# A full-width stationary for the d = 0 column, a planner without a chain of loads and with new lengths, and the third batch's folds five units later

## The chip, the cores and the metric

The kernel runs on one core of a Trainium2 chip. The metric is the device time of one execution in microseconds (us), the median of several runs. TensorE is called PE, VectorE DVE, ScalarE ACT, GpSimd POOL and SyncE SP, as in the profile.

## The reference, cut to what matters

```python
def attn(x):                       # x: (8, 3008, 256) float32
    X = np.fft.fft(x, axis=1)
    X = np.fft.fft(X, axis=2)
    return X.real                  # 24064 rows of 256

def moe(x, w_gate, w_val, w_out):  # 256 -> 1536 -> 256
    g = x @ w_gate
    silu = g * (1.0 / (1.0 + np.exp(-g)))
    val = x @ w_val
    return silu * val @ w_out
```

The output is `moe(attn(x))` in float32. Nothing but the real part of the two-dimensional transform is needed, so the kernel works with cosine and sine tables as matrix products.

## The kernel before, in words

**Folding.** The sequence transform has symmetries in both axes. POOL adds and subtracts rows of `x` (function `fold_steps`, lines 150 to 176) so that a batch is left as small coefficient tiles: `CEa` and `BBa` for the first 128 rows of a quarter (kind "A", written to one of two buffers called `cp`), and `Fc` for the remaining 60 (kind "C", for two batches at a time), which SP's DMAs spread into the stacked tile `St`. One set of folds of a kind has 12 steps, six for each `q`. Kind A reads the tile `XA`, kind C the tile `XC`; both are loaded from HBM by SP, `XA` by 20 DMAs per batch (lines 131 and 133), `XC` by 20 per batch (lines 140, 142 and 144).

**Transform.** For each of eight batches `b`, `transform_op` (line 1296) multiplies the coefficients with the tables `Tab` on PE. Part 0 has 377 output columns and part 1 has 376; each part is done for `eo` = 0 and 1, each with a product for `q` = 0 into an `o` tile in PSUM and one for `q` = 1 into a `g` tile. ACT copies the first (`od`), DVE adds and subtracts (`put`) and so writes columns of `Pt` and `Qt`, 512 columns in a tile, 24 tiles.

The column d = 0 has one coefficient more than fits in 128, so in part 0 with `eo` = 1 the function `row0` (line 586) adds three further matmuls to output row 0 alone, for each `q`: their stationary operand is 128 rows by 1 column, and they write `ps[0:1, ...]`.

**The feed-forward part.** Work goes in units `(t, f)`: tile `t` of 24, and block `f` of 12 of the 1536 hidden features, 288 units in all. In a unit PE multiplies `Pt` and `Qt` with the transformed weights `Wp`, `Wq` and `Wm` (`mm`, line 937) into the PSUM tiles `g` (gate) and `v` (value), three buffers each. Each tile also serves the mirrored rows. In the first tiles most units are "whole": DVE takes the two products with ACT's SiLU. Elsewhere they are "split": `es` (even part of the value; DVE line 1060, or ACT line 1058) and `sg` (of the gate, DVE line 1039), then `sv` (DVE line 1121 and ACT line 1107), `hp` on DVE (line 1131) and, for two units together, `hm` on POOL (`product_m`, line 1128). `es` and `sg` on DVE need a row of `Qt` spread over all partitions: for each tile, SP's DMA writes it to `br` (line 1448) and a second one to `bc` (line 1456). `OWork` multiplies `hp` and `hm` of the tile before with `Wo` (line 1177), ACT evicts (lines 1183 and 1186) and SP stores (line 1189).

**The order.** After a prologue of some 22 us, nothing is issued directly. `S.add` (line 776) records each operation with its engine, a length `dur`, the keys that it reads and writes, and a place `at`, which is the sum of PE's lengths so far plus a `shift`. A write depends on the last write of the same key and on all reads since then, and then forgets those reads. `S.run` (line 802) plays the operations in time: on each engine it takes, among those within a window of the earliest one left (2 us of `at` for PE and ACT, 3 for DVE and SP, 6 for POOL), the one that can start first. What comes out is only an order of instructions for each engine; on the chip the engines wait on semaphores. Lengths are formulas: `pe_us`, `act_us`, `dve_us` and constants.

Each of the 20 loads of `XA` for batch 1 was given, besides its own key, a write of a common one:

```python
w=[((what[0],), k)] + ([(("A",), "pre" if k > 15 else "preW")] if what == ("A", 1) else []), lat=LOAD_LAT)
```

Those two keys stand for the data that lie in the same memory before: `preW` for the raw weights, read by `weight_op`, and `pre` for angles, read by `angle_op` and `sine_op`. A load is given 10 us of latency (`LOAD_LAT`).

`spread` (line 1219) lays the 12 steps of a fold over a stretch of units. Batch 1 has its C folds in units 6 to 14 and its A folds in 15 to 24; for batch 2 the C folds went to units 25 to 44 and the A folds to 45 to 63. Transforms have a unit of their own: 33 for (batch 1, part 0), 64 for (2, 0), 88 for (3, 0), and `eo` = 1 comes one unit later.

Of the kernel before, what the change touches and what calls it, by code (L numbers as in the profile page):

```python
# [14 lines left out]
BF16 = mybir.dt.bfloat16  # L15
# [16 lines left out]
def kernel(  # L32
# [8 lines left out]
    nc = tc.nc  # L41
    B, M, D = x.shape
    Dff = moe_w_gate.shape[1]
    P = 128
    H = M // 2
    G = M // 8
# [15 lines left out]
    NCE = 2 * GH + 1  # L62
# [33 lines left out]
    SDt = const.tile([P, 2, P], BF16, name="SDt")  # L96
    m2 = const.tile([P, 1], F32, name="m2")
    mM = const.tile([P, 4], F32, name="mM")
    wC = const.tile([P, 1], F32, name="wC")
    sgn = const.tile([P, 1], F32, name="sgn")  # L100
    XA = const.tile([P, 8, 2, D], F32, name="XA")
# [85 lines left out]
    def coef_a(b):  # L187
        if b not in coefA:
            coefA[b] = (cp.tile([P, 2, 2, 2, P + 1], BF16, name="CEa"),
                        cp.tile([P, 2, 2, 2, P], BF16, name="BBa"))  # L190
        return coefA[b]
# [43 lines left out]
    q = nc.sync  # L235
# [349 lines left out]

    def row0(b, q, ps):
        CE = coef_a(b)[0]
        todo = [(CE[:, q, 0, k, P:P + 1], Tab[:, 0, q, 0, e], e) for k, e in ((0, E0), (1, E1))]
        if b:
            todo.append((stack_of(b, 0)[:, q, 0, P:P + 1], Tab[:, 1, q, 0, 0:NCE], slice(0, NCE)))  # L590
        else:
            todo += [(CEc[:, q, 0, k, 0:1], Tab[:, 1, q, 0, e], e) for k, e in ((0, E0), (1, E1))]
        for l, r_, cols in todo:
            nc.tensor.matmul(ps[0:1, cols], l, r_, start=False, stop=True, skip_group_check=True)

# [134 lines left out]
    LOAD_LAT = 10.0  # L730
# [34 lines left out]
    class Sched:  # L765
# [7 lines left out]
        def hold(self, *owner):  # L773
            self.live[owner[0]].append(owner)

        def add(self, eng, dur, fn, r=(), w=(), new=(), lat=None, shift=0.0):
            o = Op()
            o.eng, o.dur, o.fn, o.n = eng, dur, fn, len(self.ops)
            o.lat = LAG[eng] if lat is None else lat
            o.at = self.clock + shift  # L780
            if eng == "PE":
                self.clock += dur
            o.new, o.deps, o.owners = list(new), set(), set()
            for k in r:
                o.owners.add(k[0])
                if k in self.wr:
                    o.deps.add(self.wr[k])
                same = self.rd.setdefault(k, [])
                if k[0][0] in PSUM:
                    o.deps.update(x for x in same if self.ops[x].eng != eng)  # L790
                same.append(o.n)
            for k in w:
                o.owners.add(k[0])
                if k in self.wr:
                    o.deps.add(self.wr[k])
                o.deps.update(self.rd.pop(k, ()))
                self.wr[k] = o.n
            o.deps.discard(o.n)
            o.owners.update(o.new)
            self.ops.append(o)  # L800
# [96 lines left out]
        return n / 1200 + 0.055  # L897

    def dve_us(n):
        return n / 960 + 0.072  # L900

    def pool_us(n):
        return 0.16 + 1.76e-3 * n
# [109 lines left out]
    def part_a(u):  # L1013
        if whole(u):
            return whole_a(u)
        t, f = u
        w = width(t) + (B if t == nT - 1 else 0)
        kg, kv, kP, kQ = unit_keys(u)
        ksp, kes, keg = (("sp", u), 0), (("es", u), 0), (("sg", ("eg", u)), 0)
        kb = (("bc", t), 0)  # L1020

        def h():
            if t not in hts:
                hts[t] = (hp.tile([P, nF, T + B], BF16, name="hp"), hp.tile([P, nF, T], BF16, name="hm"))

        def g1():
            T_[kg] = psG.tile([P, T], F32, name="g")
            mm(T_[kg], Wp, 0, u, pq_tiles(t)[0], w, True, False)

        def g2():  # L1030
            mm(T_[kg], Wq, 0, u, pq_tiles(t)[1], w, False, True)

        def silu():
            T_[ksp] = spp.tile([P, T], F32, name="sp")
            nc.scalar.activation(T_[ksp][:, :w], T_[kg][:, :w], AF.Silu)  # L1035

        def even_gate():
            T_[keg] = sgp.tile([P, T], F32, name="sg")
            nc.vector.scalar_tensor_tensor(T_[keg][:, :w], bc[t][:, :w], w0[:, 0, f:f + 1], T_[kg][:, :w],  # L1039
                                           op0=Alu.mult, op1=Alu.add)  # L1040

        S.add("PE", pe_us(w), g1, r=[kP], w=[kg], new=[("g", u)])
        if gate_split(u):
            S.add("DVE", dve_us(w) + 0.075, even_gate, r=[kb, kg, (("w0",), 0)], w=[keg], new=[keg[0]], shift=SH_EG)
        else:
            S.add("PE", pe_us(w), g2, r=[kQ], w=[kg])
            S.add("ACT", act_us(w), silu, r=[kg], w=[ksp], new=[ksp[0]], shift=SH_SP)
        ahead = seeded(u)

        def v1():  # L1050
            if not ahead:
                T_[kv] = psV.tile([P, T], F32, name="v")
            mm(T_[kv], Wp, 1, u, pq_tiles(t)[0], w, not ahead, False)

        def even_value():
            T_[kes] = esp.tile([P, T], F32, name="es")
            if ahead:
                nc.scalar.copy(T_[kes][:, :w], T_[kv][:, :w])  # L1058
            else:
                nc.vector.scalar_tensor_tensor(T_[kes][:, :w], bc[t][:, :w], w0[:, 1, f:f + 1], T_[kv][:, :w],  # L1060
                                               op0=Alu.mult, op1=Alu.add)

        S.add("PE", pe_us(w), v1, r=[kP], w=[kv], new=[("v", u)])
        if ahead:
            S.add("ACT", act_us(w) - 0.015, even_value, r=[kv], w=[kes], new=[kes[0]], shift=SH_ES)
        else:
            S.add("DVE", dve_us(w) + 0.075, even_value, r=[kv, kb, (("w0",), 0)], w=[kes], new=[kes[0]], shift=SH_ES)

    def part_b(u):
        if whole(u):  # L1070
# [150 lines left out]

    spread(("C", 1), 12, 6, 14)
    spread(("A", 1), 12, 15, 24)
    lo = 25
    for b in range(2, B, 2):
        u = slot[(b, 0)] - 1
        spread(("C", b), 12, lo, (lo + u) // 2)
# [10 lines left out]
    def run_loads(n):  # L1238
        for what, k, fn in loads[:n]:
            S.add("SP", (0.33 if k < 16 else 0.62) if what[0] == "A" else (0.33 if k % 20 < 15 else 0.9), fn,  # L1240
                  w=[((what[0],), k)] + ([(("A",), "pre" if k > 15 else "preW")] if what == ("A", 1) else []), lat=LOAD_LAT)
        del loads[:n]

    FOLD = (("X", "F"), ("F", "E"), ("F", "O"), ("EO", "A"), ("A", "CE"), ("EO", "BB"))
# [2 lines left out]
    def fold_step(what, i, unit):  # L1247
        kind, b = what
        q, j = divmod(i, 6)
        if i == 0:  # L1250
            run_loads(max((k + 1 for k, (w_, _, _) in enumerate(loads) if w_ == what), default=0))

        def fn():
            if j == 0:
                if kind == "A":
                    queue[what] = fold_steps(nc.gpsimd, XA, *coef_a(b), q, slice(0, P))
                else:
                    if q == 0:
                        foldC[b] = fcp.tile([P, 2, 4 * ND], BF16, name="Fc")
                    F5 = foldC[b].rearrange("p k (q e n) -> p q e k n", q=2, e=2)  # L1260
                    queue[what] = fold_steps(nc.gpsimd, XC, F5[..., 0:NE], F5[..., NE:ND], q,
                                             slice(64 if b == 1 else 0, P))
            queue[what].pop(0)()

        dst = ("cp", b) if kind == "A" else ("fc", b)
        tmp = ("fold",)
        r = {0: [((kind,), k) for k in range(40)], 1: [(tmp, "F")], 2: [(tmp, "F")], 3: [(tmp, "E"), (tmp, "O")],
             4: [(tmp, "A")], 5: [(tmp, "E"), (tmp, "O")]}[j]
        w = {0: [(tmp, "F"), (tmp, "E")], 1: [(tmp, "E")], 2: [(tmp, "O")], 3: [(tmp, "A")],
             4: [(dst, (q, 0))], 5: [(dst, (q, 1))]}[j]  # L1270
        S.add("POOL", FOLD_US[j], fn, r=r, w=w, new=[dst], shift=SH_FOLD)
        if q == 1 and j == 0:
            act_at.setdefault(max(unit + LOAD_AT, 15), []).append(what)
        if kind == "C" and q == 1 and j == 5:
            spread_at[unit + 2] = b

    def load_next(what):
        kind, b = what
# [17 lines left out]
    def transform_op(b, part, eo):  # L1296
# [3 lines left out]
        kd = (("od", (b, part, eo)), 0)  # L1300
        coef = [(("cp", b), (q, part)) for q in range(2)] + [(("st", b), k) for k in range(2)]
        coef += [(("Tab",), k) for k in ((("o", 0), ("o", 1)) if not b else ("k", "z"))]
        us = 0.5 if part == 0 else 0.42
        extra = 0.2 if part == 0 and eo else 0.0
        S.add("PE", us + extra, todo["q0"], r=coef, w=[ko], new=[ko[0]])
        S.add("ACT", act_us(n), todo["od"], r=[ko], w=[kd], new=[kd[0]], shift=SH_OD)
        S.add("PE", us + extra, todo["q1"], r=coef, w=[kg], new=[kg[0]])
# [101 lines left out]
    def rows_op():  # L1409
# [9 lines left out]
        S.add("PE", 0.7, product, r=[(("Wq",), (fc, gv)) for fc in range(1, 3) for gv in range(2)], w=[ko], new=[ko[0]])  # L1419
        S.add("ACT", 0.15, lambda: nc.scalar.copy(w0.rearrange("p g f -> p (g f)"), T_[ko][:, 0:2 * nF]), r=[ko], w=[(("w0",), 0)])  # L1420

    def halve_tables():
        nc.gpsimd.memset(Tab[0:64, 1, :, :, GH + 1:NCE], 0.0)
        nc.gpsimd.memset(Tab[64:P, 1, :, :, 0:GH + 1], 0.0)
# [6 lines left out]
    def odd_op(i):  # L1431
# [3 lines left out]
              4: [lambda: weight_op(2, 0), lambda: angle_op(1)], 5: [lambda: weight_op(2, 1), lambda: cosine_op(1)],  # L1435
              7: [lambda: sine_op(0), rows_op], 8: [lambda: sine_op(1)], 9: [weigh_op],
              13: [lambda: odd_op(0)], 14: [lambda: odd_op(1)], 15: [lambda: odd_op(2)], 16: [lambda: odd_op(3)],
              17: [lambda: S.add("POOL", 0.8, halve_tables, w=[(("Tab",), "z")])]}

    def row_width(t):  # L1440
        return width(t) + (B if t == nT - 1 else 0)
# [115 lines left out]
```

## Time and profile before

| | |
|---|---|
| median of 3 runs | 612.57 us (612.53 to 613.61) |
| span of the profiled execution | 611.4 us, 12521 instructions |
| PE busy | 599.6 us (98%) |
| DVE busy | 581.1 us (95%) |
| ACT busy | 526.4 us (86%) |
| POOL busy | 470.8 us (77%) |
| granted PE clock | 1.000 |

The profile is of one execution, and gives its span from the first to the last instruction; no time of its own stands beside it. The median of the runs is 1.2 us above that span, and what lies around the span is taken to stay the same. Matmuls overlap in the records, so a busy PE need not be one at its peak; the starts of its matmuls tell more.

### The profile page before, as it was taken

The page shows a single profiled execution, that of the slowest core. Times are in us where ns is not written, and L with a number is a line of the kernel's source. Part 1 is how long each engine was busy: PE and PEld are TensorE (multiplying, and loading weights), DVE is VectorE, ACT ScalarE, POOL GpSimd, SP SyncE. Part 2 cuts the span into 40 slices and gives each one's busy share as a digit, 9 for nine tenths or more (in the row PEclk, how much of TensorE's full clock was granted, in tenths as well). Part 3 has the DMA queues.
Part 4 walks back from the last instruction along what each step waited for, and adds up shares of the span by engine and source line. Part 5 has one row for each costly group of instructions (what it writes and reads, how often), then busy time and mean ns, then how long its engine had stood idle before and what let it go on. Part 6 is the DMA issues. An engine that isn't in the chain of part 4 may idle for free. (4 is left out here: it accounts for less than half of the span.)

```text
span 611.4 us, 12521 instructions
## 1 busy us (share of the span) xinstructions
PE 599.6 (98%) x4028; PEld 394.2 (64%) x4088; DVE 581.1 (95%) x1073; ACT 526.4 (86%) x1003; POOL 470.8 (77%) x427
## 2 busy tenths in 40 slices
PE   8999999999999999999999999999999999999997
PEld 6555666666666666666666666666666666666686
DVE  8999899999999999999999999999999999999992
ACT  7686567999989889889999899998898988999994
POOL 8869999999787999977987869867886444446652
PEclk9999999999999999999999999999999999999999
DMA  9957447445425223464152113134211111111212
GB/s 226 144 100 137 126 112 172 116 139 129 133 53 150 70 65 105 136 130 132 45 155 79 54 45 96 53 92 127 62 55 43 49 59 47 51 43 55 59 53 79
DMA packets 50736, 57.71 MB, mean 94 GB/s; under 512 B 7256, under 2 KB 37724, under 8 KB 50670
## 3 DMA queue, kind: packets, MB, share of 16 engines
q1 hardware_dynamic: 47016, 53.78, 33.3%
q0 software_dynamic: 3216, 2.36, 2.9%
q10 hardware_dynamic: 438, 0.77, 0.5%
q8 instruction: 32, 0.52, 0.4%
q14 instruction: 34, 0.28, 0.2%
HBM read 29.43 MB, written 24.65 MB: 88 GB/s over the span
## 5 line engine op out<-in xcount | busy, mean ns | idle before, releaser
L1128 POOL TENSOR_TENSOR hm<-sv 128x1024 bf16<-128x1024 f32 (+2 forms) x135 | 251.0, 1860 | 112.0 <-ACT sv L1107 63.7
L1121 DVE SCALAR_TENSOR_TENSOR sv<-es,v 128x512 f32<-128x512 f32 (+2 forms) x270 | 181.4, 673 | 2.8 <-PE v L937 1.7
L1131 DVE TENSOR_TENSOR hp<-sp,v 128x512 bf16<-128x512 f32 (+2 forms) x264 | 177.7, 673 | 3.9 <-ACT sp L1104 2.1
L1177 PE MATMUL o<-Wo,hm 128*128 128x256 bf16 (+1 forms) x1128 | 167.1, 273 | 0.6
L1177 PE MATMUL o<-Wo,hp 128*128 128x256 bf16 (+1 forms) x1104 | 165.3, 273 | 0.4
L1177 PEld LDWEIGHTS <-hm 128*128 128x128 bf16 (+2 forms) x1140 | 111.9, 98 | 62.0 <-issue 0.2
L1035 ACT ACTIVATE sp<-g 128x512 f32<-128x512 f32 (+2 forms) x205 | 122.6, 598 | 33.0 <-PE g L937 20.7
L1177 PEld LDWEIGHTS <-hp 128*128 128x128 bf16 (+2 forms) x1140 | 112.0, 98 | 58.9 <-issue 1.1
L1107 ACT ACTIVATE sv<-g 128x512 f32<-128x512 f32 (+2 forms) x205 | 133.2, 651 | 8.1 <-PE g L937 3.8
L937 PE MATMUL v<-Pt,Wp 128*128 128x512 bf16 (+2 forms) x283 | 106.2, 375 | 1.3 <-DVE sv L1121 0.4
L1060 DVE SCALAR_TENSOR_TENSOR es<-bc,w,v 128x512 f32<-128x512 bf16 (+2 forms) x144 | 105.5, 734 | 1.2 <-PE v L937 0.8
L937 PE MATMUL g<-Pt,Wp 128*128 128x512 bf16 (+2 forms) x284 | 106.5, 375 | 0.1
L937 PE MATMUL g<-Qt,Wq 128*128 128x512 bf16 (+2 forms) x246 | 92.1, 374 | 0.3
L1009 ACT ACTIVATE v<-bc,w 128x512 f32<-128x512 bf16 (+2 forms) x126 | 86.9, 690 | 0.4
L937 PE MATMUL g<-Qt,Wm 128*128 128x512 bf16 (+2 forms) x215 | 80.6, 375 | 0.4
L1058 ACT COPY es<-v 128x512 f32<-128x512 f32 (+2 forms) x126 | 73.6, 584 | 3.0 <-PE v L937 2.8
L937 PEld LDWEIGHTS <-Wp 128*128 128x128 bf16 x576 | 56.1, 98 | 29.5 <-issue 4.3
L937 PE MATMUL v<-Qt,Wq 128*128 128x512 bf16 (+2 forms) x162 | 60.7, 375 | 2.1 <-DVE es L1060 1.7
L937 PEld LDWEIGHTS <-Wq 128*128 128x128 bf16 x450 | 43.9, 98 | 22.2 <-issue 1.4
L1183 ACT COPY ev<-o 128x512 f32<-128x512 f32 x89 | 53.3, 599 | 4.0 <-PE o L1177 2.7
L937 PE MATMUL v<-Qt,Wm 128*128 128x512 bf16 (+2 forms) x144 | 53.9, 374 | 0.2
L1039 DVE SCALAR_TENSOR_TENSOR sg<-bc,w,g 128x512 f32<-128x512 bf16 (+2 forms) x65 | 47.6, 733 | 1.2 <-ACT sg L972 0.6
(196 smaller groups left out, 682.9 us busy)
## 6 DMA issues: line engine op xcount, KB each, us to landing
out_dram<-ev SPq DMA_DIRECT2D x96, 128.0 KB
XA<-in_x_dram SPq DMA_DIRECT2D x30, 256.0 KB
XA<-in_x_dram SPq DMA_DIRECT2D x112, 64.0 KB
XC<-in_x_dram SPq DMA_DIRECT2D x30, 120.0 KB
XC<-in_x_dram SPq DMA_DIRECT2D x105, 32.0 KB
bc<-br SPq DMA_DIRECT2D x21, 128.0 KB
St<-Fc SPq DMA_DIRECT2D x14, 128.5 KB
out_dram<-ev SPq DMA_DIRECT2D x12, 120.0 KB
```

The source lines that it names most:

```text
L937: nc.tensor.matmul(ps[:, :n], Wt[:, gv, fs], src[:, :n], start=start, stop=stop, skip_group_check=True)
L1009: nc.scalar.activation(T_[kv][:, :w], bc[t][:, :w], AF.Copy, scale=w0[:, 1, f:f + 1])
L1035: nc.scalar.activation(T_[ksp][:, :w], T_[kg][:, :w], AF.Silu)
L1039: nc.vector.scalar_tensor_tensor(T_[keg][:, :w], bc[t][:, :w], w0[:, 0, f:f + 1], T_[kg][:, :w], op0=Alu.mult, op1=Alu.add)
L1058: nc.scalar.copy(T_[kes][:, :w], T_[kv][:, :w])
L1060: nc.vector.scalar_tensor_tensor(T_[kes][:, :w], bc[t][:, :w], w0[:, 1, f:f + 1], T_[kv][:, :w], op0=Alu.mult, op1=Alu.add)
L1107: nc.scalar.activation(sv()[:, f % 2, w - 1::-1, 1], T_[kgm if by_dve else kg][:, :w], AF.Silu)
L1121: nc.vector.scalar_tensor_tensor(sv()[:, f % 2, w - 1::-1, 0], T_[kes][:, :w], 2.0, T_[kv][:, :w], op0=Alu.mult, op1=Alu.subtract)
L1128: nc.gpsimd.tensor_tensor(hts_(t)[1][:, f - 1:f + 1, :w], sv()[:, :, :w, 1], sv()[:, :, :w, 0], op=Alu.mult)
L1131: nc.vector.tensor_tensor(hts_(t)[0][:, f, :wp], T_[ksp][:, :wp], T_[kv][:, :wp], op=Alu.mult)
L1177: nc.tensor.matmul(st["ps"][:n, j, :], hts[t][minus][:, f, c:c + n], Wo[:, f, :], start=(f == 0), stop=(f == nF - 1))
L1183: nc.scalar.copy(ev[:, 0:len(pair), :], st["ps"][:, 0:len(pair), :])
```

## The change

`row0` uses, for every batch but the first, a tile `Z0` of 128 columns per matmul that is zero except for its first column, and writes all 128 rows of the PSUM tile. POOL clears `Z0` once, in unit 6, and copies the coefficients into it after the last A fold of each batch (`d0_op`, two copies per batch). `S.add` gets an argument `after`: it depends on the reads of a key without writing it, and the loads of batch 1 use it in place of the common writes. `dve_us` loses 7 ns and the operations that read `bc` another 15; the lengths of a transform on PE are worked out from its columns. The folds from batch 2 on start at unit 30 where they started at 25, so that the C folds of batch 2 lie in units 30 to 46 and its A folds in 47 to 63.

```diff
+    Z0 = const.tile([P, 2, 3, P], BF16, name="Z0")
...
     def row0(b, q, ps):
         CE = coef_a(b)[0]
+        if b:
+            for k, (c, e) in enumerate(((0, E0), (0, E1), (1, slice(0, NCE)))):
+                nc.tensor.matmul(ps[:, e], Z0[:, q, k, :], Tab[:, c, q, 0, e], start=False, stop=True,
+                                 skip_group_check=True)
+            return
         todo = [(CE[:, q, 0, k, P:P + 1], Tab[:, 0, q, 0, e], e) for k, e in ((0, E0), (1, E1))]
-        if b:
-            todo.append((stack_of(b, 0)[:, q, 0, P:P + 1], Tab[:, 1, q, 0, 0:NCE], slice(0, NCE)))
-        else:
-            todo += [(CEc[:, q, 0, k, 0:1], Tab[:, 1, q, 0, e], e) for k, e in ((0, E0), (1, E1))]
+        todo += [(CEc[:, q, 0, k, 0:1], Tab[:, 1, q, 0, e], e) for k, e in ((0, E0), (1, E1))]
...
-        def add(self, eng, dur, fn, r=(), w=(), new=(), lat=None, shift=0.0):
+        def add(self, eng, dur, fn, r=(), w=(), new=(), after=(), lat=None, shift=0.0):
...
+            for k in after:
+                o.deps.update(self.rd.get(k, ()))
...
     def dve_us(n):
-        return n / 960 + 0.072
+        return n / 960 + 0.065
...
-            S.add("DVE", dve_us(w) + 0.075, even_gate, r=[kb, kg, (("w0",), 0)], w=[keg], new=[keg[0]], shift=SH_EG)
+            S.add("DVE", dve_us(w) + 0.06, even_gate, r=[kb, kg, (("w0",), 0)], w=[keg], new=[keg[0]], shift=SH_EG)
...
-            S.add("DVE", dve_us(w) + 0.075, even_value, r=[kv, kb, (("w0",), 0)], w=[kes], new=[kes[0]], shift=SH_ES)
+            S.add("DVE", dve_us(w) + 0.06, even_value, r=[kv, kb, (("w0",), 0)], w=[kes], new=[kes[0]], shift=SH_ES)
...
-    lo = 25
+    lo = 30
     for b in range(2, B, 2):
...
-                  w=[((what[0],), k)] + ([(("A",), "pre" if k > 15 else "preW")] if what == ("A", 1) else []), lat=LOAD_LAT)
+                  w=[((what[0],), k)], after=[(("A",), "pre" if k > 15 else "preW")] if what == ("A", 1) else [], lat=LOAD_LAT)
...
+        if kind == "A" and q == 1 and j == 5:
+            for part in range(2):
+                d0_op(b, part)
...
-        us = 0.5 if part == 0 else 0.42
-        extra = 0.2 if part == 0 and eo else 0.0
+        us = 3 * 0.0025 + (2 * NCE / 2400 if part == 0 else 3 * G / 2400)
+        extra = us if part == 0 and eo else 0.0
+        if extra:
+            coef += [(("Z0",), k) for k in range(2)]
...
+    def clear_d0():
+        nc.gpsimd.memset(Z0, 0.0)
+
+    def d0_op(b, part):
+        def fn():
+            if part:
+                nc.gpsimd.tensor_copy(Z0[:, :, 2, 0:1], stack_of(b, 0)[:, :, 0, P:P + 1])
+            else:
+                nc.gpsimd.tensor_copy(Z0[:, :, 0:2, 0:1], coef_a(b)[0][:, :, 0, :, P:P + 1])
+
+        r = [(("st", b), k) for k in range(2)] if part else [(("cp", b), (q, 0)) for q in range(2)]
+        S.add("POOL", 0.16, fn, r=r, w=[(("Z0",), part)])
...
+              6: [lambda: S.add("POOL", 0.5, clear_d0, w=[(("Z0",), k) for k in range(2)])]}
```

## The prediction

> **What bounds the kernel now.** I read the page first. PE is the busiest engine:
>
> ```profile
> PE 599.6 (98%) x4028; PEld 394.2 (64%) x4088; DVE 581.1 (95%) x1073; ACT 526.4 (86%) x1003; POOL 470.8 (77%) x427
> ```
>
> Records of matmuls overlap, so I went to the windows to see where PE falls short (columns: window, its length, then busy time of PE, PEld, DVE, ACT and POOL with counts, granted clock, DMA share and GB/s):
>
> ```profile
> 23.00:106.00 83.00, 79.99 (x506) 47.80 (x512) 78.30 (x139) 58.44 (x111) 76.32 (x90) 1.00 0.65 135
> 106.00:579.00 473.00, 470.22 (x3135) 308.67 (x3187) 463.14 (x826) 431.56 (x818) 362.72 (x290) 1.00 0.31 85
> ```
>
> From 106 to 579 us PE lacks 2.8 us of 473, and the list of waits has no row of PE there except its weight loads. I then took starts of matmuls in the timeline. A 512-column matmul is followed by the next start after 216 ns, which is 512 columns at 2.4 per ns plus 2.7 ns; a 256-column one after 109. Wherever the spacing exceeds this by a whole matmul, two weight loads stand in the gap, so a record is missing (60 of 4088 are). What is left in that stretch is one pattern, at the single-column matmuls of line 594:
>
> ```profile
> 424.59 0.32 PE L1320 MATMUL o<-Tab,St 128*128 128x377 bf16 x1
> 424.84 0.33 PE L594 MATMUL o<-Tab,CEa 128*1 128x189 bf16 x2
> 425.01 0.32 PE L594 MATMUL o<-Tab,St 128*1 128x377 bf16 x1
> 425.26 0.39 PE L937 MATMUL v<-Pt,Wp 128*128 128x512 bf16 x1
> ```
>
> A 377-column matmul takes 377/2.4 = 157 ns of array time; from 424.59 to 424.84 is 250 ns, and from 425.01 to 425.26 again. So going into the narrow stationary costs about 95 ns and coming out another 95. Real waits of PE, outside the prologue, are few and early:
>
> ```profile
> PE v L937 <- DVE es L1060: 1.7, 2, 0.9
> PE v L937 <- DVE sv L1121: 0.4, 1, 0.4
> ```
>
> These end at 54.68, 74.02 and 78.68 us. So: PE sets the pace throughout, and only two kinds of time can be won without less work, the switches and the early waits.
>
> **Row 0 with 128 columns.** Seven batches, two `q`: 14 visits. The 14 entries exceed array time by 1.32 us together, the 14 exits by 1.42, of which one (at 93.83) contains 0.08 of another wait. Without a switch each of the 28 steps would still have 3 ns: 0.08. That leaves 1.32 + 1.34 - 0.08 = 2.58 us. What is added: a 128-column weight load in place of a 1-column one (98 against 82 ns in PEld's rows), under short matmuls. The same pair of shapes with 128 columns stands in line 1320: 189 to 188 columns exceeds array time by 3.7 ns, 188 to 377 by 7.2; in line 594 it is 2.3 and 6.1. So 2.5 ns by 14 = 0.04 us. Matmul lengths are equal (243 to 246 ns and 321 in both). Sum **-2.5 us**, all on the path, because no other engine is late in that stretch. Bounds: -2.6 (weight loads quite hidden) and -2.0 (loads exposed by 98 - 79 = 19 ns behind each of the 28 short matmuls, 0.5 us).
>
> The Trainium skill, "TensorE: Matmul & The Clock Gate", section "LDWEIGHTS", speaks against this: a weight load takes the number of columns divided by 1.2, so 107 ns for 128 columns and almost nothing for one. By it a 128-column load under a 78 ns matmul would show 29 ns, an estimate of 0.8 us over 28 short matmuls, and the sum would be -1.7. The trace differs at both ends (82 ns for one column, and 3.7 to 7.2 ns shown at line 1320). For the switch itself, "TensorEngine Tiling (Array Packing)", section "Key Properties", says that changing the tiling mode drains TensorE; the 95 ns agree.
>
> **POOL's copies.** Fourteen small copies; the nearest row is line 557 (`EOA<-SA`, 128x8, 189 ns): 2.6 us of POOL, with 0.5 for clearing `Z0`. The clearing lies in POOL's idle time before 42.27. The copies are in front of PE: row 0 waits for both, and behind them in POOL's queue stand the `hm` products. In the profile of before the last step of batch 2's A folds ends at 148.71 and row 0 starts at 157.16; for batches 3, 4 and 6 the distance is 8 to 9 us too, and larger for 5 and 7. One or two `hm` of 1.85 us each fit between. I take 0; if the copy comes behind two more `hm`, 0 to 2 us at batch 2.
>
> **The planner's loads.** With the common write, each of 16 loads waited in the plan for the load before it, 10.3 us each: some 165 us in a plan where the A folds of batch 1 were meant for units 15 to 24. Loads, folds and all that POOL does behind them were therefore planned far too late, and PE, ACT and DVE were ordered around a stop that the chip never had. On the chip POOL was simply in arrears: it works without a break from 42 to 117 us, and fold steps meant for unit 25 (PE reaches it at 74 us) start at 87.49. Waits of PE between 50 and 106 us, from spacing: 1.00 at 53.46; 0.09 + 1.04 + 0.19 + 0.57 from 72.58 to 78.68; 0.40 in small pieces from 91 to 106. Together 3.3 us, the most that a better order can win. The wait at 53.46 stems from two table copies ahead of `es` on DVE (2.42 us from 51.42, planned at 0.8 each), which the change leaves. The 78.68 one stems from `sv` waiting for POOL's `hm`, whose arrears stay. I take 1.0 of the 1.9 us from 72 to 79: **-1.0**, with 0 to -3.3 as bounds for what is won.
>
> What it costs: SP's order. Before, it was
>
> ```profile
> 35.77 6.96 SPq L131 DMA_DIRECT2D XA<-in_x_dram  x8
> 44.74 0.61 SPq L1448 DMA_DIRECT2D br<-Qt  x1
> 45.40 1.51 SPq L131 DMA_DIRECT2D XA<-in_x_dram  x4
> 47.01 0.61 SPq L133 DMA_DIRECT2D XA<-in_x_dram  x1
> 47.71 0.58 SPq L1456 DMA_DIRECT2D bc<-br  x1
> ```
>
> Free of the chain, all 16 loads of line 131 are due no later than `br` and go first: at 0.87 us each (6.96/8) they end at 49.7, and `bc` moves by up to 5 us, to 52.7. DVE's first `es` started at 53.88; behind `es` on DVE stand `sv` and `hp`, and PE waits for it already. If loads go at the 0.38 us of the second group, nothing is late. I take +0.3, bounds 0 and +2.
>
> **Lengths and unit 30.** The new DVE lengths are 598 ns at 512 columns and 658 with `bc`; starts in the trace are 598 and 658 apart. The plan becomes truer, and nothing changes on the chip except by order. From 106 us there is nothing to win. Moving the folds to unit 30 lets `hm` go first while POOL is in arrears: unit 30 is reached by PE at about 85 us, POOL ends batch 1's folds at 85.69. Four half sets then need about 33 us of folds and 30 of `hm` in 33 units of 2.06 us = 68 us, 93% of POOL; they end near 150, as before. 0 us.
>
> **Sum.** -2.5 - 1.0 + 0.3 = -3.2: a span of 608.2 us where it was 611.4; the median of the runs stands 1.2 above that span, so **609.4 us**.
>
> **Rivals.** (A) *Only the switches go*; the early order merely exchanges one wait for another. For it: the waits stem from POOL's arrears and the table copies, which stay. Time 612.6 - 2.5 = 610.1, up to 611.3 with small new waits. (B) *The row loads come late*: `bc` 5 us later stops DVE's queue at its first `es`, 2 us, and nothing else is won: 612.1; range 611.2 to 613. Against it: those loads were slow only until 43 us. (C) *Slower: DVE loses its margin.* Adding up starts, DVE needs 97 to 98% of each stretch from 98 to 498 us. The old lengths held 27 x 7 + 9 x 22 ns = 0.4 us of reserve per tile (operations of a steady tile); without it the plan lets DVE run later, and if PE waits 0.25 us in each of 21 tiles, that is +5.2: 612.6 - 2.5 + 5.2 = 615.3. It decides from 0.18 us per tile. Against it: PE waits nowhere in 473 us, so order has slack to spare, and the lengths now equal the trace. (D) *The 95 ns do not belong to the column count* but to leaving the product's group or to the small output; then they stay: 612.5. Against: line 1416, also one column, shows 96 and 92 at its ends, while line 1320 to 937 shows 5.
>
> **Chances.** Forecast 0.52, A 0.22, B 0.13, C 0.10, D 0.03. 0.2% is 1.2 us, about what this measurement can tell. Faster: forecast, A and a little of B, 0.76; same: most of B and D, 0.14; slower 0.10. The range starts where all early waits vanish (612.6 - 2.5 - 3.3 = 606.8) and ends at 612.4, within B, leaving out C, D and the end of B.
>
> **What would show it.** Right: line 594 keeps only the prologue's eight narrow matmuls, row 0 follows line 1320 without 95 ns, `PEld L594 <- issue` goes to about 0.5 us; waits of PE from 72 to 79 shrink. Wrong: a PE wait on POOL's `Z0` near a transform, a `bc` landing after 54 us with DVE idle before `es`, or PE waits on `es` and `sv` after 106 us.

## The result and the profile after

The changed kernel is slower, by about as much as the measurement can tell. The median of 20 runs is 615.25 us (613.56 to 618.1), that of the kernel before, timed beside it 20 times, 613.24 us; the ratio is 1.0028, with a 95% interval of 1.0015 to 1.0041. The prediction was 609.4 us with a range of 606.8 to 612.4, so it was wrong in sign, and the time lies above its range. The profiled execution took 616.86 us, 1.76 above its span of 615.1; it is among the longer ones (its granted clock is 0.994, as in 5 others of the 20; 13 have 0.997 and spans of 612.2 to 614.0, one has 0.999).

The head of the page looks harmless (columns as before, and 15 POOL instructions more):

```profile
PE 602.7 (98%) x4088; PEld 397.2 (65%) x4088; DVE 580.3 (94%) x1073; ACT 528.4 (86%) x1003; POOL 473.4 (77%) x442
```

The windows of the changed kernel (length, busy time of PE, PEld, DVE, ACT and POOL with counts, granted clock, DMA share, GB/s) show that the loss lies early. I cut the worst stretch out of the first:

```profile
23.00:106.00 83.00, 76.63 (x477) 45.66 (x476) 73.35 (x130) 55.26 (x104) 70.10 (x85) 0.96 0.60 133
106.00:579.00 473.00, 472.67 (x3194) 311.38 (x3194) 463.42 (x828) 432.41 (x816) 368.29 (x307) 1.00 0.31 85
52.00:57.90 5.90, 0.43 (x3) 0.12 (x2) 0.82 (x2) 1.05 (x3) 5.74 (x7) 0.82 0.31 79
57.90:62.70 4.80, 4.80 (x18) 2.62 (x18) 4.22 (x7) 0.96 (x2) 4.39 (x7) 0.51 0.41 110
```

In the third row PE, DVE and ACT all stand still for more than 4 of 5.9 us; in the fourth PE is fully busy, at half the clock. (The 472.67 of the second row is not better than the 470.22 of before: that trace lacked 60 records of matmuls, this one none.) The list of waits from 23 to 106 us (who waited for whom: us in total, times, the longest) names who was late:

```profile
PE v L942 <- DVE es L1065: 5.5, 1, 5.5
DVE es L1065 <- DMA bc<-br: 5.4, 1, 5.4
```

SP's part of the timeline (start, length, line, transfer, count) shows why `bc` was late. Compare it with the five lines of before in the prediction:

```profile
36.80 10.09 SPq L132 DMA_DIRECT2D XA<-in_x_dram  x16
47.20 2.60 SPq L134 DMA_DIRECT2D XA<-in_x_dram  x4
49.90 0.55 SPq L1472 DMA_DIRECT2D br<-Qt  x1
54.66 0.57 SPq L1480 DMA_DIRECT2D bc<-br  x1
```

All 20 loads now stand ahead of tile 1's row. `br` is issued 5.2 us later (49.90 against 44.74). It also takes longer: `bc`, which waits for its landing, is issued 4.8 us behind it, where it was 3.0 (in e1 and e3 below, 3.5 behind 12 loads and 3.8 behind 20). So `bc` comes 7.0 us later, and DVE's first `es` runs into it, then PE:

```profile
57.08 1.41 DVE L1065 SCALAR_TENSOR_TENSOR es<-bc,w,v 128x512 f32<-128x512 bf16 x2 [5.40 <-DMA bc<-br]
```

```profile
52.03 0.38 PE L942 MATMUL g<-Qt,Wq 128*128 128x512 bf16 x1
57.88 0.58 PE L942 MATMUL v<-Qt,Wq 128*128 128x512 bf16 x1 [5.47 <-DVE es L1065]
58.26 0.63 PE L942 MATMUL v<-Pt,Wp 128*128 128x512 bf16 x1
```

The starts 57.88, 58.26 and 58.69 (the next matmul) are 380 to 430 ns apart, where 512 columns take 216.

What was meant to be won was won. The timeline of PE at a transform after the change has no gap around row 0:

```profile
429.68 0.32 PE L1330 MATMUL g<-Tab,St 128*128 128x377 bf16 x1
429.84 0.49 PE L591 MATMUL g<-Tab,Z 128*128 128x189 bf16 x3
430.17 0.38 PE L942 MATMUL g<-Pt,Wp 128*128 128x512 bf16 x1
```

From 429.68 to 429.84 is 160 ns for 157 of array time, where it was 250.

**Where the time went.** For each kernel in the table I added up what the starts of PE's matmuls exceed their array time (columns / 2.4 per ns, plus 2.6 ns). "Rest" is the span without the prologue, whose length varies by itself between 21.8 and 23.4 us. The other columns are its excess in us: the switches into and out of narrow stationaries, the extra of matmuls at half clock (told by their doubled spacing where the granted clock is down), and waits by stretch of time. `e1` and so on are the experiments below.

```
kernel            span   rest   switches half  <50  50-70 70-106 106-580 >580
before           611.36 588.83   2.69   0     2.02  1.00  2.26   0.08   0.17
after            615.09 593.19   0.09   2.09  2.11  5.82  0.69   1.92   0.02
e1_loads11       610.69 588.68   0.09   0     2.01  0.40  3.84   1.86   0.02
e2_z0            609.49 587.22   0.09   0     2.07  0.56  2.78   1.20   0.08
e3_nochain       616.38 594.59   2.69   1.68  2.54  5.63  1.17   0      0.24
e4_chain         611.41 589.12   0.09   0     2.03  1.46  3.28   1.81   0.02
e5_len           612.06 589.69   2.69   0     2.06  0.49  3.25   0.78   0.02
e6_lo30          611.53 589.24   2.70   0     2.35  1.25  2.08   0.06   0.18
e13_oldlen       608.97 586.16   0.09   0     2.33  1.44  0.82   1.15   0.08
e15_halve6       611.00 588.44   0.09   0     2.04  0.28  3.90   2.10   0.02
e16_z0_halve6    610.68 587.25   0.09   0     2.03  1.49  1.93   1.17   0.08
```

After less before, in the two profiled executions: switches -2.60, waits from 50 to 70 us +4.82, half clock +2.09, 70 to 106 us -1.57, 106 to 580 us +1.84, the end -0.15, prologue -0.63, all else -0.1: +3.7 us. The medians differ by 2.0 only; that most executions have a clock of 0.997 and not 0.994 fits that.

### The profile page after: what moved, and what is told of

Same layout as the page of the kernel before. It is cut to its first block, busy times and chain, and to the rows that moved or that the text cites. A ratio compares the mean times of both kernels' runs of the same rounds, so it can differ in the third digit from the quotient of the medians.

```text
span 615.1 us, 12630 instructions
## 1 busy us (share of the span) xinstructions
PE 602.7 (98%) x4088; PEld 397.2 (65%) x4088; DVE 580.3 (94%) x1073; ACT 528.4 (86%) x1003; POOL 473.4 (77%) x442
## 4 chain that ended last, share of the span: by engine, by line
PE 90%; DMA 3%; ACT 3%; DVE 3%; issue 1%; SPq 0%; POOL 0%; ACTq 0%; DVEq 0%
PE o L1182 37%; PE g L942 26%; PE v L942 19%; PE o L1330 2%; PE g L1330 2%; DMA XC<-in_x_dram 1%; DMA XA<-in_x_dram 1%; DMA br<-Qt 1%; ACT sp L1040 1%; ACT sv L1112 1%; PE v L1182 1%; DVE hp L980 0%; DVE sv L1126 0%; DVE hp L1136 0%; ACT v L1014 0%
## 5 line engine op out<-in xcount | busy, mean ns | idle before, releaser
L1112 ACT ACTIVATE sv<-g 128x512 f32<-128x512 f32 (+2 forms) x205 | 135.5, 662 | 17.0 <-PE g L942 16.8
L1040 ACT ACTIVATE sp<-g 128x512 f32<-128x512 f32 (+2 forms) x205 | 125.0, 610 | 21.8 <-PE g L942 21.2
L942 PE MATMUL v<-Pt,Wp 128*128 128x512 bf16 (+2 forms) x288 | 108.1, 375 | 0.3 <-DVE hm L1000 0.2
L942 PE MATMUL g<-Pt,Wp 128*128 128x512 bf16 (+2 forms) x288 | 108.1, 375 | 0.0
L942 PE MATMUL g<-Qt,Wq 128*128 128x512 bf16 (+2 forms) x288 | 108.0, 375 | 0.0
L942 PE MATMUL g<-Qt,Wm 128*128 128x512 bf16 (+2 forms) x223 | 83.7, 375 | 0.6 <-ACT sp L1040 0.4
L1109 ACT ACTIVATE sp<-g 128x512 f32<-128x512 f32 (+2 forms) x65 | 38.3, 590 | 13.1 <-DVE sg L1104 13.1
```

What stands on the lines that cost most here:

```text
L942: nc.tensor.matmul(ps[:, :n], Wt[:, gv, fs], src[:, :n], start=start, stop=stop, skip_group_check=True)
L1109: nc.scalar.activation(T_[ksp][:, :wp], T_[kg][:, :wp], AF.Silu)
L1112: nc.scalar.activation(sv()[:, f % 2, w - 1::-1, 1], T_[kgm if by_dve else kg][:, :w], AF.Silu)
```

## The experiments

Each was timed in five rounds against the kernel before.

**Put the row's place back: e1.** Theory 1: the order of SP's queue is all that is wrong, and the loss is `bc`. The changed kernel, with eight of batch 1's 20 loads given to the planner later:

```diff
-        if i == 8:
+        if i == 11:
             loads[0:0] = ... load_a(1, ...)
```

> The changed kernel, with the loads of batch 1's XA entering the plan at unit 11 where they enter at 8; in SP's order twelve loads then stand ahead of tile 1's br and bc, and eight behind. Theory 1 (tile 1's row is late because 20 loads stand ahead of it; PE waits 5.6 us and then runs some 5 us at half clock): the wait falls to 1 us or so, the clock stays at 1.000, the span goes from 615.1 to about 608.5, 3 us under the kernel before. Theory 2 (the new order itself is worse, by its lengths and by the folds from unit 30, with some 2.4 us of small waits of PE between 106 and 579 us): the long wait goes too, but the span stays at 611 or above, no better than before.

Median 612.28 against 613.2, ratio 0.999 (0.9966 to 1.0014). SP's timeline in this kernel:

```profile
36.72 8.51 SPq L132 DMA_DIRECT2D XA<-in_x_dram  x12
45.69 0.61 SPq L1472 DMA_DIRECT2D br<-Qt  x1
49.14 0.63 SPq L1480 DMA_DIRECT2D bc<-br  x1
```

The long wait and the half clock are gone: 7.5 us less in the table's two columns. So the cause of the early loss is the queue's order. But only 4.4 us of span came back, less than theory 1 asked for, because a wait of 2.5 us appeared at 75.68 that neither kernel had in that length. In the timeline of e1:

```profile
73.19 2.35 POOL L158 TENSOR_TENSOR SDf<-XA 128x1020 f32<-128x1020 f32 x1
...
75.65 1.89 POOL L1133 TENSOR_TENSOR hm<-sv 128x1024 bf16<-128x1024 f32 x1
...
77.58 1.29 DVE L1126 SCALAR_TENSOR_TENSOR sv<-es,v 128x512 f32<-128x512 f32 x2 [2.33 <-POOL hm L1133]
78.32 0.38 PE L942 MATMUL v<-Pt,Wp 128*128 128x512 bf16 x1 [2.36 <-DVE sv L1126]
```

Read upwards: PE waits for `sv` on DVE, that for a buffer which `hm` on POOL must free, and `hm` stands behind a fold step of batch 1. This is POOL's arrears, which the prediction knew (in the kernel before, the wait at this place was 0.57 us). In the changed kernel it does not show: POOL worked 5.74 of the 5.9 us in which PE stood still. That POOL caught up by this was read from the trace, not tested; e13 below shows that POOL's lateness alone does not make the 2.5 us.

**Each part alone: e3, e2, e5, e6.** The kernel before, with only `after=` in place of the common writes:

```diff
+            for k in after:
+                o.deps.update(self.rd.get(k, ()))
...
-                  w=[((what[0],), k)] + ([(("A",), ...)] if what == ("A", 1) else []), lat=LOAD_LAT)
+                  w=[((what[0],), k)], after=[(("A",), ...)] if what == ("A", 1) else [], lat=LOAD_LAT)
```

> The kernel before with the planner's loads freed of their chain, nothing else. Theory 1: the long wait for tile 1's row is there in full, 5 to 6 us with a clock under 1 behind it, the waits from 72 to 79 us are gone, and the time is 3 to 6 us above the kernel before. Theory 2: without the new lengths and unit 30 there is little harm: within 1.5 us of the kernel before.

Median 617.0 against 613.2, ratio 1.0043 (1.002 to 1.0067): this part alone costs 0.4%, as theory 1 expected (3.8 us). Its `br` and `bc` come later still than in the changed kernel, and PE's clock falls in the same way (SP's timeline, then the window behind the wait):

```profile
48.77 2.61 SPq L133 DMA_DIRECT2D XA<-in_x_dram  x4
51.48 0.54 SPq L1450 DMA_DIRECT2D br<-Qt  x1
55.29 0.57 SPq L1458 DMA_DIRECT2D bc<-br  x1
```

```profile
58.50:63.00 4.50, 4.46 (x17) 2.55 (x17) 4.26 (x7) 1.31 (x3) 4.09 (x5) 0.53 0.40 109
```

Compared with the kernel before, ACT's order of instructions is the same, and PE's differs in 32 places, DVE's in 7, POOL's in 8 and SP's in 11 of its 626 transfers. So the false chain had shaped few places of any order but SP's. One of them counts. In the kernel before, PE lost 1.04 us to `es` at 74.02:

```profile
74.02 0.38 PE L937 MATMUL v<-Qt,Wq 128*128 128x512 bf16 x1 [0.88 <-DVE es L1060]
```

This wait, 1.04 us each time, and one of 0.18 to 0.19 us some 2 us behind it stand in all six kernels that keep the chain and the old `SH_FOLD` (before, e2, e4, e5, e6, e16). In the seven without the chain (the changed kernel, e1, e3, e7, e8, e13, e15) neither is there.

Only row 0 with `Z0` (`row0`, `clear_d0`, `d0_op` and the dependency of the transform on it):

```diff
+        if b:
+            ... nc.tensor.matmul(ps[:, e], Z0[:, q, k, :], ...)
+            return
```

> The kernel before with the 128-column stationary alone (tile Z0, its clearing and its copies on POOL); the planner, its lengths and unit 25 as before. Theory 1 and theory 2: 2.5 us faster than before (28 switches of 95 ns gone), with PE's early waits where they were. If the 95 ns do not belong to the column count: no difference. If POOL's copies stand in front of PE: slower, with a PE wait at a transform.

Median 612.1 against 613.2, ratio 0.9977 (0.9956 to 0.9999). The switches are 2.60 less, but the span without its prologue fell by 1.61 only, not by the 2.5 expected: 1.12 came back as small waits from 106 to 580 us, although PE's order, row 0 itself apart, differs in 4 places, ACT's in 4, DVE's in 6. One of these waits, in the timeline of e2:

```profile
366.55 0.68 ACT L1038 ACTIVATE sp<-g 128x512 f32<-128x512 f32 x1
366.68 0.38 PE L940 MATMUL g<-Pt,Wp 128*128 128x512 bf16 x1
...
366.89 0.38 PE L940 MATMUL g<-Qt,Wq 128*128 128x512 bf16 x1
...
367.29 0.38 PE L940 MATMUL g<-Qt,Wm 128*128 128x512 bf16 x1
```

From 366.89 to 367.29 is 400 ns where 216 are usual. ACT's SiLU ends at 367.23, and then PE goes on. The same place in the kernel before:

```profile
367.91 0.70 ACT L1035 ACTIVATE sp<-g 128x512 f32<-128x512 f32 x1
368.47 0.38 PE L937 MATMUL g<-Qt,Wq 128*128 128x512 bf16 x1
368.69 0.38 PE L937 MATMUL g<-Qt,Wm 128*128 128x512 bf16 x1
```

There the SiLU ends at 368.61, 80 ns before PE takes its next matmul at the usual pace. PE has three `g` tiles and needs the one that this SiLU frees: the pauses of 95 ns, four to a batch, had given ACT that time, and without them PE runs into it. This was read from the timelines at one such place (others, of 0.11 to 0.21 us, are at 172.6, 294.4, 439.3 and 511.7, before the same kind of matmul); the list of waits names no cause for them.

Only the new lengths (`dve_us`, the 0.06 of `es` and `sg`, those of a transform):

```diff
-        return n / 960 + 0.072
+        return n / 960 + 0.065
```

> The kernel before with the new DVE and transform lengths alone. Theory 2 (the lengths take away a reserve): small waits of PE of 0.5 to 1 us in sum appear between 106 and 579 us, where there were 0.1, and the time rises by as much. Rival (these waits belong to the shorter transforms of the 128-column stationary): none appear, same time within 0.5 us.

Median 613.58 against 613.45, ratio 0.9986 (0.9963 to 1.0009): no difference in time, but 0.70 us more of small waits from 106 to 580 us, and 1.0 more from 70 to 106 with 0.5 less from 50 to 70. These lengths change the order far more than the chain did: PE's in more than 400 places, ACT's in 144.

Only the folds from unit 30 (`lo = 30`):

> The kernel before with the folds from unit 30 alone. Expected by theory 1: within 0.7 us of the kernel before; by theory 3 PE's waits from 87 to 106 us move (0.4 us before) but are not gone. If unit 30 is what makes the waits of 0.6 and 0.5 us near 100 and 105 us that the changed kernel and the first experiment show: 0.7 to 1.2 us slower.

Median 612.8 against 613.45, ratio 0.9981 (0.9955 to 1.0008), with 3.33 us of waits from 50 to 106 us where the kernel before has 3.26. No effect; and since no other edit is in it, 0.2% is a fair measure of what two kernels of one speed can show here.

**The chain put back: e4.** The changed kernel with the old line in `run_loads`:

> The changed kernel with the chain put back, nothing else. Theory 1: tile 1's row is early again, the clock is 1.000, and the time is 2.5 to 3 us under the kernel before. Theory 2: the small waits after 106 us stay, and the time is between 1 us under and 1 us above the kernel before.

Median 612.48 against 613.2, ratio 0.9989 (0.9968 to 1.0011). `br` goes out at 44.31, `bc` at 47.26, `es` starts at 54.11, and the clock stays at 1.0. The row and the clock are as theory 1 said, the time and the waits as theory 2 said: the loss is gone, but waits of 3.28 us from 70 to 106 and 1.81 behind take most of what the switches gave.

**Is the half clock an effect of the idle time? e7.** The changed kernel, where unit (1, 4) repeats its first two products twelve more times, 24 matmuls or 5.2 us of work in the time that PE would wait:

```diff
+            again = 13 if u == (1, 4) else 1
+            for i in range(again):
+                if i:
+                    mm(T_[kg], Wp, 0, u, pq_tiles(t)[0], w, True, False)
                 mm(T_[kg], Wq, 0, u, pq_tiles(t)[1], w, False, True)
```

> The changed kernel, in which PE does the two gate matmuls of unit (1, 4), the last ones ahead of its long wait, twelve times more (24 matmuls of 216 ns, 5.2 us, with the same result). The wait for tile 1's row is as long as before, but PE is busy in it. Theory 1a (the idle wait makes the clock drop, and half clock costs another 2.1 us behind it): the wait of PE shrinks to 0.5 to 1 us, the clock is 1.000, and though PE does 5.2 us more work the span is 2 us shorter than the changed kernel's 615.1: 613. Theory 1b (matmuls are spaced wide there for another reason, for instance that the engines behind them start from empty queues): the wide spacing stays and the span is 615 or more.

Median 615.04 against 613.45, ratio 1.0012 (0.9986 to 1.0038). The same two windows as above, in e7, and DVE's first `es`:

```profile
52.00:57.90 5.90, 5.85 (x33) 3.04 (x32) 0.49 (x1) 1.72 (x3) 5.74 (x6) 1.00 0.50 119
57.90:62.70 4.80, 4.80 (x32) 3.08 (x31) 4.55 (x8) 2.33 (x4) 4.39 (x6) 1.00 0.27 73
```

```profile
58.11 1.40 DVE L1069 SCALAR_TENSOR_TENSOR es<-bc,w,v 128x512 f32<-128x512 bf16 x2 [5.62 <-DMA bc<-br]
```

`es` waits for `bc` as long as in the changed kernel (5.62 against 5.40 us), but PE kept working, and the clock stays at 1.00 behind it: 32 matmuls in the 4.8 us that held 18. Its span without the prologue is 591.1 us against 593.2. So the half clock follows from PE's standing still, and cost 2.1 us beside the wait in the profiled execution; in the medians, where most executions of the changed kernel have 0.997 and not 0.994, less of it shows (615.04 and 615.25).

**The waits at 76 and later: e8, e15, e16, e12, e13.** e8 is e1 with batch 1's A folds spread over units 15 to 29 instead of 15 to 24:

> The changed kernel with XA's loads from unit 11, as in the first experiment, and the A folds of batch 1 spread over units 15 to 29 where they took 15 to 24. Theory 3 (between 50 and 106 us POOL is the bound: with the row in time, PE waits 3.8 us in all for POOL's hm behind fold steps): hm gets in between, the 2.5 us wait at 75.7 goes, and the span falls by 1.5 to 2.5 us, to 608.2 to 609.2. Rival (POOL's work is only moved: the arrears return before the transform): the sum of waits from 50 to 106 us stays at 4 us, span 610.7.

Median 612.7 against 613.45, ratio 0.9975 (0.9948 to 1.0001). A wait of 2.80 us stays at 76.5, since the fold step and `hm` kept their order on POOL at that place: the expectation missed. e15 is e1 with `halve_tables` moved from unit 17 to 6 of the list of extra work, which takes its work out of POOL's busy time:

> The first experiment's kernel (the change, with XA's loads from unit 11) with POOL's clearing of the table halves (two memsets, 1.45 us) moved from unit 17 to unit 6, into POOL's idle time near 37 to 42 us; the order of PE and DVE is the same instruction by instruction. Theory 3 (POOL's arrears are what PE waits for between 50 and 106 us): every POOL step behind is 1.45 us earlier, PE's 2.5 us wait at 75.7 shrinks to 1.1, the span falls by about 1.4 us to 609.3. Rival (the wait stems from DVE's or ACT's order): no change, 610.7.

Median 612.64 against 613.5, ratio 0.9974 (0.9952 to 0.9997). PE's waits from 45 to 110 us, first in e1 and then in e15:

```profile
PE v L942 <- DVE sv L1126: 2.4, 1, 2.4
PE g L942 <- ACT sp L1040: 0.4, 1, 0.4
PE v L942 <- ACT v L1014: 0.4, 1, 0.4
```

```profile
PE v L942 <- ACT v L1014: 1.4, 1, 1.4
PE v L942 <- DVE sv L1126: 0.9, 1, 0.9
PE g L942 <- ACT sp L1040: 0.8, 1, 0.8
```

The wait on `sv` shrank by 1.5 us, as expected, and the two on ACT, at 99.3 and 104.8, grew by 1.4: the sum from 50 to 106 stayed at 4.2. The gain was given back later, and the 1.4 us of span that was expected did not come. e16 does the same to e2:

> The kernel before with the 128-column stationary alone and the same two memsets moved to unit 6. Theory 3: of PE's 3.3 us of waits from 50 to 106 us those on POOL go (0.6 near 77 us, part of the 0.4 and 0.4 near 94 and 97), 0.6 to 1.2 us in sum; span 608.3 to 608.9, time 1 us under the 128-column stationary alone and 2 to 3 us under the kernel before. Rival: no change, span 609.5.

Median 612.32 against 613.5, ratio 0.9973 (0.995 to 0.9996). 0.85 us less from 70 to 106, 0.93 more from 50 to 70: nothing won, so the expectation missed. e12 is e2 with the folds' `shift` (`SH_FOLD`) at 0 instead of -2, so that `hm` goes ahead of them:

> The kernel before with the 128-column stationary alone, and fold steps planned two units of 1 us later (their shift 0 in place of -2), so that hm goes ahead of them more often. Theory 3: waits on POOL between 70 and 106 us shrink, span 608.5 to 609.3. Rival (folds then end later and the transforms wait for them): new waits at transforms, span 609.5 to 612.

Median 613.02 against 613.5, ratio 0.9998 (0.9972 to 1.0023). The waits are 2.88 us from 70 to 106 and 1.80 behind, against 2.78 and 1.20 in e2: nothing won. Last, e13 is e1 with the old lengths of DVE and of the transforms:

> The first experiment's kernel (the change, with XA's loads from unit 11) with the old lengths of DVE's operations and of the transforms. Theory 2b (the new lengths give 0.8 us of the 1.9 us of small waits from 106 to 579 us, the faster transforms the other 1.0): 0.9 to 1.1 us of waits left there, span 0.8 us under the first experiment's, 609.9. Rival (they come from the order without the chain): still 1.9 us there.

Median 611.6 against 613.5, ratio 0.9956 (0.9927 to 0.9985): the fastest of the study, and with the interval farthest below 1. Its windows, as above:

```profile
23.00:106.00 83.00, 80.74 (x513) 48.87 (x520) 80.32 (x142) 60.48 (x112) 75.99 (x91) 1.00 0.61 137
106.00:579.00 473.00, 470.09 (x3145) 311.79 (x3197) 464.24 (x829) 432.52 (x821) 367.04 (x305) 1.00 0.31 85
```

Against e1, the waits from 106 to 580 us fell from 1.86 to 1.15, and those from 50 to 106 from 4.24 to 2.26. (The PE column can't be compared: this trace lacks 62 records.) So 0.7 of the small waits behind 106 us belong to the lengths, as e5 showed from the other side (0.70), and 1.1 to the freed switches (e2): together the 1.84 found.

The early part tells more. POOL's steps hardly moved against e1: the `hm` at 75.65 there stands at 75.41 here. Yet PE waits 0.27 us at this place, at 78.09, where it waited 2.53; it has waited 1.44 us from 50 to 70 instead of 0.40. Only the lengths differ, so the 2.5 us wait of e1 needs the order that the new lengths give PE. And the 2.26 us from 50 to 106 are 1.0 less than in the kernel before (3.26), while `Z0` alone (3.34) and unit 30 alone (3.33) take nothing off. What is left is the freed loads with eight of them behind the row, or the parts together; the loads were not run by themselves in this place.

## Why the prediction was wrong

**Row 0: right in its own size.** -2.5 was taken and -2.60 measured, at the end of the bounds at which weight loads are hidden: the spacing at row 0 exceeds array time by 1 to 8 ns. By the Trainium skill's rule ("TensorE: Matmul & The Clock Gate", "LDWEIGHTS"), an estimate of 0.8 us of the loads would have shown; it did not. One piece of evidence was misread: the matmuls of line 1416 have a stationary of 1 row by 128 columns, not of one column, so their 96 and 92 ns are no evidence on the column count. It is e2 that answers rival D. POOL's copies cost 0.19 and 0.20 us each (lines 1438 and 1440, at 85.68) and PE never waited for them. **Unit 30: right**, 0 (e6).

**"What it costs: SP's order": the step that failed.** It was priced at +0.3 with bounds of 0 and +2, and measured 4.82 us of wait and 2.09 of half clock in the profiled execution. The mechanism was seen, also in rival B, and among the signs of being wrong; its terms were mis-sized. `br` itself went out when it was forecast, at 49.90 against 49.7, but by luck: the four loads of line 133 (2.60 us), which the prediction left behind `br`, went ahead too, and the 16 of line 131 took 10.09 us in place of 13.9. Three things then made the wait. First, `bc` was shifted by its issue alone, as if `br` would land as fast behind the loads as before; that took 4.8 us in place of at most 3.0, so `bc` was issued at 54.66 and not at 52.7. Second, 52.7 is an issue, and was held against the start of `es`; `es` starts 2.4 us behind the issue of `bc` (57.08). Even the forecast issue would have meant 55.1. Third, I took 53.88, the start of DVE's first `es`, as the due time, and said that the change leaves the two table copies ahead of it. DVE in the kernel before, then in the changed one:

```profile
51.42 2.42 DVE L1429 COPY Tab<-Tab 64x752 bf16<-64x752 bf16 x2
53.88 1.41 DVE L1060 SCALAR_TENSOR_TENSOR es<-bc,w,v 128x512 f32<-128x512 bf16 x2
```

```profile
49.66 1.43 DVE L1452 COPY Tab<-Tab 64x752 bf16<-64x752 bf16 x2
51.01 0.67 DVE L1000 TENSOR_TENSOR hm<-sg,v 128x512 bf16<-128x512 f32 x1
```

The copies moved: DVE has nothing left from 51.7, and `bc` was needed by then. So the 1.2 us that the forecast issue would have cost (55.1 against 53.88) grew by 2.0 for the landing of `br` and by 2.2 for the due time, to 5.4. The half clock was not priced at all: a wait of this length is not worth its length alone.

**"The planner's loads", -1.0: right at its place, not in the sum.** The premise was too strong: without the chain the orders of PE, ACT and DVE are nearly the same (e3). But the wait at 74.02, of which the -1.0 was taken, is gone in every kernel without the chain. What the prediction missed is that the other wait, at 78.68, need not stay at 0.57 us. In the changed kernel it is not there, behind the long wait; with the row in time and the new lengths it is 2.53 (e1), more than what was won; with the old lengths 0.27 (e13).

**"From 106 us there is nothing to win": true, but there was something to lose,** 1.84 us. 1.1 of it is the switches' own gain, given back (e2) where PE runs into ACT; I had taken -2.5 as "all on the path, because no other engine is late in that stretch". Not late is not the same as having slack. The other 0.7 is the lengths' loss of reserve: rival C in kind, at 0.03 us per tile (0.7 / 21) in place of 0.25. The switches' net gain is 1.6 us (e2). With the row in its place the whole change comes out as rival A in kind, and at less than its gain: the medians of e1 and e4 lie 0.9 and 0.7 us below before, and neither is clear of noise. With the old lengths as well (e13) it is 1.9 us.

**Open:** why the new lengths lose 0.5 us (e5) to 2.0 (e1 against e13) from 50 to 106 us; PE's order differs in too many places to name one. Also whether the freed loads alone, with the row in time, win the 1.0 us of e13. That the two waits at 99 and 105 us stem from ACT's work on `Wm` standing ahead of its SiLU was read from the timeline and not tested.

## What to carry to other kernels

A false dependency in a planner can hold an order that matters: before removing one, list what it keeps behind what in each queue, and look above all for a small transfer of two hops that the freed bulk transfers will now precede. Take a transfer's due time from when its reader has nothing else left to do, not from when the reader started. On an engine that is 98% busy beside two others at 86 and 95%, a pause that is removed can be worth less than its length (here 1.6 of 2.60 us), unless the next engine has been shown to have slack.

## What the runs showed of the hardware

A wait of PE of 5.6 us brought 6.8 us at half clock, which cost another 2.1 us. The windows of the changed kernel around it:

```profile
52.00:55.74 3.74, 0.41 (x2) 0.10 (x1) 0.00 (x0) 1.05 (x3) 3.71 (x4) 1.00 0.34 89
55.74:62.57 6.83, 4.69 (x17) 2.51 (x17) 5.04 (x8) 0.83 (x2) 6.30 (x9) 0.50 0.36 95
```

The clock fell some 3.5 us into the wait, and came back 4.7 us after PE had begun to work again. In e3 it was at half for 6.83 us too, from 55.86 to 62.69; the window in front of that:

```profile
52.50:55.86 3.36, 0.91 (x7) 0.49 (x5) 0.00 (x0) 0.89 (x2) 3.36 (x4) 1.00 0.46 144
```

The wait of 2.5 us in e1 is followed by no half clock:

```profile
75.90:78.20 2.30, 0.05 (x1) 0.00 (x0) 0.62 (x2) 0.62 (x2) 2.30 (x2) 1.00 0.48 145
78.20:82.00 3.80, 3.68 (x24) 2.25 (x23) 3.16 (x7) 3.28 (x8) 3.80 (x4) 1.00 0.24 77
```

The Trainium skill ("TensorE: Matmul & The Clock Gate", "What's actually happening") says that the clock is halved after an idle window of 3.4 us that runs freely. The 6.83 us agree: they are two such windows. In e3, though, the clock fell 2.6 us after PE's last matmul, and PE had been busy for 0.91 of the 3.36 us before the fall. So the window need not be wholly idle; the 2.8 us wait of e8 brought no half clock, and where the limit lies no run shows. The 13 timed runs with 0.997 fit one window (0.003 x 614 x 2 = 3.7 us), the six with 0.994 two, which is an estimate from rounded clocks. That the same wait costs one window or two would explain why the changed kernel's executions spread as they do. It is not shown: of the 35 runs of the kernel before that stand beside e1, four have 0.997 as well, and only the profiled execution tells where its clock fell.

Behind bulk transfers issued by the same engine, a small transfer paid twice here: `br` waited 5.2 us for the issue of the loads, and then landed in 4.8 us (3.8 in e3, 4.7 in e7, all behind 20 loads; 3.5 in e1 behind 12) in place of at most 3.0 behind 8. I had expected the first and not the second.

Row 0 shows what a narrow stationary costs: about 95 ns going in and 95 coming out between 128-column ones, 2.60 us in 28 steps, and nothing of it with the same column in a tile of 128 (e2).
